# Seven-for-eight up product from the third chunk on, with the cell's steps placed anew beside it

## The chip, the cores and the metric

The kernel runs on one core of a Trainium2 chip. The core has a matrix engine (TensorE, PE in the profile; its weight loads are listed as PEld), three engines for element-wise work (VectorE or DVE, ScalarE or ACT, GpSimd or POOL), and a queue engine (SyncE or SP) that starts most of the DMA transfers. The engines run at the same time, each takes its instructions in order, and they wait for each other by semaphores. The metric is the device time of one execution in microseconds (us); all times here are in us unless marked ns.

## The reference

An mLSTM cell over 4 batches, 8 heads, 768 steps and head dimension 40, and then a feed-forward layer with the activation h·cos(h) over the 3072 rows of 320 that come out of it.

```python
def _attn_ref(q, k, v, i_gate, f_gate, o_gate):
    for t in range(S):
        m_new = np.maximum(f_gate[:, :, t] + m, i_gate[:, :, t])
        f_stab = np.exp(f_gate[:, :, t] + m - m_new)
        i_stab = np.exp(i_gate[:, :, t] - m_new)
        C = f_stab * C + i_stab * (v_t outer k_t)
        n = f_stab * n + i_stab * k_t
        h_tilde = C @ q_t
        denom = np.maximum(np.abs(n . q_t), 1.0)
        y[:, :, t] = sigmoid(o_gate[:, :, t]) * h_tilde / denom

def _moe_ref(x, w_in, w_out):       # x (3072, 320), w_in (320, 2048), w_out (2048, 320)
    h = x @ w_in
    g = h * np.cos(h)
    return (g @ w_out).astype(np.float32)
```

The loop body is shortened here: indices that only spread a value over dimensions are left out.

## The kernel before

**Tiling.** The 768 steps are cut into NC = 6 chunks of C = 128. A *cell* is one chunk of one batch with all eight heads; cells are numbered n = chunk · 4 + batch, 24 in all. Within a cell the recurrence is written as a masked product: scores (keys times queries), weighed with exponentials of the gates, values, and a state that goes on to the next chunk. The feed-forward layer works on the finished chunk: 512 rows (4 batches of 128) by 2048 columns of w_in, in NF / 2 = 8 *up slots* of two blocks of 128 columns. Everything is float32. A float32 matmul shows as two records in the profile.

**The order.** It is written out by hand. `both_parts(c, b)` (line 1265) lays chunk c's up slots 2b and 2b + 1 beside cell n = (c + 1) · 4 + b, which belongs to the next chunk. Two slots with what lies beside them are a *period* here: its first part (i = 0) is the even half, its second (i = 1) the odd half. A chunk has four periods, b = 0 to 3. For c = 5 there is no cell left, and the cells beside c = 4 (n = 20 to 23) no longer add to the state: no `seam`, `fade` and `state` there.

**A slot** (class `Up`, line 697): two banks of 128 by 512 in PSUM get two products each over 128 rows of x (line 715) and one over the 64 remaining rows, the *low rows* (line 709); the two low products use the two halves of the array side by side. Odd slots do the low rows first. Then cos is taken as a sine: ScalarE rounds (`near`, line 723), VectorE takes the rest (`rest`, 726), ScalarE the sine (`sin`, 731), VectorE multiplies by h and 2π (`gate`, 735). e = 0 and 1 are the two banks.

**Seven for eight.** The last chunk (`fast = NC - 1`, line 742) uses `UpFast` (line 769): the product of two blocks of columns with two halves of the rows over two blocks of x, eight products of 256 columns, is done in seven from sums of weights (`up_weight_sums`) and of x (`x_sums`, GpSimd, before the chunk). Four products fill the banks; ScalarE copies both banks out (lines 788, 789); two *filling* products of the down layer (`fill_in`, from f2 = 2 on) lie between; three more products and the low rows go on top. Three adds of the copies (797 and 799 on GpSimd, 798 on VectorE), then two *bank adds* on VectorE (800, 802) give h.

**The down layer.** From chunk 1 on it is a product of the same kind, from sums of the gated values (`sums`, lines 868 to 871, VectorE) and sums of w_out. `down_slot` (line 1031) runs a quota of its products behind each slot: 12 of the chunk before at f2 = 0, 16 *late* ones at f2 = 1, 14 at f2 = 2 to 7 (less two filling ones). `combine_first`, `combine` and `combine_late` add the parts up into output tiles.

**The cell's steps in a period before.** Even half: `scores` right behind the low rows; `weigh` (536) on VectorE; `decay` (448), the eight exponentials of the next cell on ScalarE; behind the slot's down products `values` (556 to 565) and `seam` (the state's increments, 667); then `normalize_turned`, the division on VectorE, which starts with line 583 and ends with 604 and writes the next chunk's x; `fade` (650, GpSimd). Odd half: `state` (692) ahead of the gates, `weigh_k`, and at its end `turn_blocks` (508), two transposes on VectorE that make the next cell's keys and queries for its `scores`, and `scale_q` (512, GpSimd). The exponentials, the sigmoid and the sine are in different tables of ScalarE, so a switch shows as a table load; `sin_next` loads the sine's early.

The end of the even half and of the odd one before, cut:

```python
            down_slot(c, f2)
            if cell and i == 0:
                values(n)
                seam(n)
                normalize_turned(n)
                fade(n)
                sin_next()
            if f2 == 0 and c > 1:
                for p in range(2):
                    combine(c - 1, p)
            if i == 1:
                turn_blocks(n + 1)
                scale_q(n + 1)
```

Of the kernel before, what the change touches and what calls it, by code (L numbers as in the profile page):

```python
# [29 lines left out]
def kernel(  # L30
# [410 lines left out]
    def decay(n):  # L441
        c, b = divmod(n, B)
        if n < B:
            nc.scalar.activation(out=Es[n], in_=Es[n], func=AF.Exp, scale=-1.0)
            return
        for h in range(H):
            g = b * H + h
            nc.scalar.activation(out=Es[n][:, h], in_=Es[n][:, h], func=AF.Exp, scale=-1.0, bias=tab[:, c, 0, g:g + 1])  # L448
# [248 lines left out]
    class Up:  # L697
# [35 lines left out]
        def gate(self, e):  # L733
            g = gp.tile([128, B * C], FP, name="g", tag="g")
            nc.vector.scalar_tensor_tensor(out=g, in0=self.pu[e], scalar=TWO_PI, in1=self.n[e].bitcast(FP),  # L735
                                           op0=OP.mult, op1=OP.mult)
            gs[self.c, 2 * self.f2 + e] = g
# [4 lines left out]
    fast = NC - 1  # L742
    Sw, Tx = {}, {}

    def up_weight_sums(part):

        tt = nc.gpsimd.tensor_tensor
        if part == 0:
            S1, S2, S4, S3 = Sw.setdefault(0, [*(room[:, i] for i in range(3)), blocks[:, FREE_AT:FREE_AT + NF // 2]])
            tt(out=S1, in0=A21, in1=A22, op=OP.add)  # L750
            tt(out=S2, in0=S1, in1=A11, op=OP.subtract)
        else:
            S1, S2, S4, S3 = Sw[0]
            tt(out=S3, in0=A11, in1=A21, op=OP.subtract)
            tt(out=S4, in0=A12, in1=S2, op=OP.subtract)

# [4 lines left out]
    def x_sums(c):  # L761
        T1, T2, T4 = Tx[c] = pe.tile([128, H, C], FP, name="Tx", tag="E")[:, 0:3 * B // 2].rearrange("p (k b) t -> k p b t", k=3)
# [6 lines left out]
    class UpFast(Up):  # L769


        def __init__(self, c, f2, fill):
# [14 lines left out]
            s = pe.tile([128, H, C], FP, name="Sx", tag="E").rearrange("p (k b) t -> p k (b t)", k=4)  # L787
# [10 lines left out]
            nc.vector.tensor_tensor(out=s[:, 0], in0=s[:, 0], in1=s[:, 3], op=OP.add)  # L798
            nc.gpsimd.tensor_tensor(out=s[:, 3], in0=s[:, 1], in1=s[:, 2], op=OP.add)
            nc.vector.tensor_tensor(out=b0[:, second], in0=b0[:, second], in1=s[:, 0], op=OP.add)  # L800
            h = s[:, 0:4:3]
            nc.vector.tensor_tensor(out=h, in0=b1.rearrange("p (k n) -> p k n", k=2), in1=h, op=OP.add)
            self.n = [p3.tile([128, B * C], I32, name="n", tag="n") for _ in range(2)]
            self.h = h

        def near(self, e):
            if e == 0:
                return super().near(e)
            nc.scalar.activation(out=self.n[e].rearrange("p (k n) -> p k n", k=2), in_=self.h, func=AF.Copy, bias=0.25)

        def rest(self, e):
            if e == 0:
                return super().rest(e)
            n = self.n[e].rearrange("p (k n) -> p k n", k=2)
            nc.vector.scalar_tensor_tensor(out=n.bitcast(FP), in0=self.h, scalar=0.25, in1=n, op0=OP.add, op1=OP.subtract)

        def gate(self, e):
            if e == 0:
                return super().gate(e)
            g = gp.tile([128, B * C], FP, name="g", tag="g")  # L820
            nc.vector.scalar_tensor_tensor(out=g.rearrange("p (k n) -> p k n", k=2), in0=self.h, scalar=TWO_PI,
                                           in1=self.n[e].rearrange("p (k n) -> p k n", k=2).bitcast(FP), op0=OP.mult, op1=OP.mult)
            gs[self.c, 2 * self.f2 + e] = g

    def down(c, f2):
# [6 lines left out]
        for f, b in order:  # L832
            nc.tensor.matmul(po[c][b], gs[c, f][:, ts(b, C)], w_out_sb[:, f], start=(f == 0), stop=(f == NF - 1))  # L833
            if f == NF - 1:
                o = out_tile()
                nc.scalar.copy(out=o, in_=po[c][b])
# [4 lines left out]
    T, acc, late, outs_of = [None] * 3, {}, {}, {}  # L841

# [19 lines left out]
    def sums(c, k):  # L862
# [4 lines left out]
        tt = nc.vector.tensor_tensor  # L867
        tt(out=S2_D1, in0=G0[:, :, 1], in1=G1[:, :, 1], op=OP.add)
        tt(out=S0_S1, in0=S2_D1, in1=G0[:, :, 0], op=OP.subtract)
        tt(out=S3_D4, in0=G1[:, :, 0], in1=S0_S1, op=OP.subtract)  # L870
        tt(out=G0[:, :, 1], in0=G0[:, :, 0], in1=G0[:, :, 1], op=OP.subtract)
# [9 lines left out]
    def products(c, k):  # L881
# [6 lines left out]
        made = [(X0, 0, G0[:, 0, 0], B11), (X0, 1, G1[:, 0, 0], B21), (X0, 2, S[:, 0], T2),  # L888
                (Y0, 0, G0[:, 0, 1], T3), (Y0, 1, G1[:, 0, 1], T4), (Y0, 2, S[:, 2], T1),
                (Y1, 2, S[:, 3], B22),  # L890
                (X1, 0, G0[:, 1, 0], B11), (X1, 1, G1[:, 1, 0], B21), (X1, 2, S[:, 1], T2),
                (Y1, 0, G0[:, 1, 1], T3), (Y1, 1, G1[:, 1, 1], T4)]
# [56 lines left out]
    def combine_last():  # L949
        c = NC - 1  # L950
        X0, X1, Y0, Y1 = acc[c]
        tt = nc.vector.tensor_tensor
        lo, hi = slice(0, HALF), slice(HALF, DM)

        def spread_first(X):
            o = [out_tile() for _ in range(2)]
            nc.scalar.copy(out=o[1][:, lo], in_=X[:, 0])
            tt(out=o[0].rearrange("q (h n) -> q h n", h=2), in0=X[:, 1:3], in1=o[1][:, lo].unsqueeze(1).to_broadcast([128, 2, HALF]), op=OP.add)
# [3 lines left out]
        tt(out=o[1][:, hi], in0=Y0[:, 0], in1=o[0][:, hi], op=OP.add)  # L962
        tt(out=o[1].rearrange("q (h n) -> q h n", h=2), in0=Y0[:, 1:3], in1=o[1][:, hi].unsqueeze(1).to_broadcast([128, 2, HALF]), op=OP.add)
        out_to(c, 1, o[1])
        tt(out=o[0][:, hi], in0=Y0[:, 2], in1=o[0][:, hi], op=OP.add)
        p = spread_first(X1)
        tt(out=o[0][:, hi], in0=Y1[:, 1], in1=o[0][:, hi], op=OP.add)
        out_to(c, 0, o[0])
        o, L = p, late[c]
        tt(out=o[1][:, lo], in0=Y1[:, 0], in1=o[0][:, hi], op=OP.add)  # L970
        tt(out=o[1][:, hi], in0=L[:, 0], in1=o[1][:, lo], op=OP.add)
        tt(out=o[0][:, hi], in0=L[:, 0], in1=o[0][:, hi], op=OP.add)
        tt(out=o[0][:, hi], in0=L[:, 1], in1=o[0][:, hi], op=OP.add)
        out_to(c, 2, o[0])
        tt(out=o[1][:, lo], in0=own[c], in1=o[1][:, lo], op=OP.add)
# [12 lines left out]
    def combine_first(c, p):  # L988

        o = outs_of[c, p] = [out_tile() for _ in range(2)]  # L990
        nc.scalar.copy(out=o[1][:, 0:HALF], in_=acc[c][p][:, 0])

    def combine(c, p):

        X0, X1, Y0, Y1 = acc[c]
        X, Y = (X0, Y0) if p == 0 else (X1, Y1)
        tt = nc.vector.tensor_tensor
        o = outs_of[c, p]
        tt(out=o[0].rearrange("q (h n) -> q h n", h=2), in0=X[:, 1:3], in1=o[1][:, 0:HALF].unsqueeze(1).to_broadcast([128, 2, HALF]), op=OP.add)
        if p == 0:  # L1000
            tt(out=o[1][:, HALF:DM], in0=Y[:, 0], in1=o[0][:, HALF:DM], op=OP.add)
            tt(out=o[1].rearrange("q (h n) -> q h n", h=2), in0=Y[:, 1:3], in1=o[1][:, HALF:DM].unsqueeze(1).to_broadcast([128, 2, HALF]), op=OP.add)
            tt(out=o[0][:, HALF:DM], in0=Y[:, 2], in1=o[0][:, HALF:DM], op=OP.add)
            tt(out=o[0][:, HALF:DM], in0=Y1[:, 2], in1=o[0][:, HALF:DM], op=OP.add)
            for e in range(2):
                out_to(c, e, o[e])
        else:
            tt(out=o[1][:, HALF:DM], in0=Y[:, 0], in1=o[0][:, HALF:DM], op=OP.add)
            tt(out=o[1][:, 0:HALF], in0=Y[:, 1], in1=o[1][:, HALF:DM], op=OP.add)

    def combine_late(c):
        tt = nc.vector.tensor_tensor
        o, L = outs_of[c, 1], late[c]
        tt(out=o[0][:, HALF:DM], in0=L[:, 0], in1=o[0][:, HALF:DM], op=OP.add)
        tt(out=o[1][:, HALF:DM], in0=L[:, 0], in1=o[1][:, HALF:DM], op=OP.add)
        tt(out=o[0][:, HALF:DM], in0=L[:, 1], in1=o[0][:, HALF:DM], op=OP.add)
# [6 lines left out]

    def fill_in(c, f2):

# [388 lines left out]
```

## Time and profile before

| | us |
|---|---|
| median of 3 runs | 523.0 (521.36 to 523.67) |
| the profiled execution | 521.93 |
| its span, first to last instruction | 520.2 |
| TensorE clock granted | 1.00 of full speed |

The span is cut into stretches by the start of a chunk's first up product. Columns: length, busy time of TensorE, VectorE, ScalarE, GpSimd.

| stretch | us | PE | DVE | ACT | POOL |
|---|---|---|---|---|---|
| chunk 2 (204.58 to 284.79) | 80.21 | 80.21 | 65.03 | 44.72 | 18.45 |
| chunk 5 and the last products (443.01 to 508.69) | 65.68 | 65.35 | 48.17 | 28.83 | 11.80 |

A busy time is the sum of an engine's instructions in the stretch, with overlaps counted once. TensorE's ends are modelled, and a matmul's record overlaps the next one's; what a product costs is read from the distance between starts. Chunks 3 and 4 are shown in the prediction.

### The profile page before, as it was taken

To read this page: it belongs to the slowest core of one execution; us is meant where nothing else is said; L and a number is where in the kernel's file an instruction comes from. 1 tells how busy PE (TensorE), PEld (TensorE's weight loads), DVE (VectorE), ACT (ScalarE), POOL (GpSimd) and SP (SyncE) were. 2 spreads that over 40 slices of the span, in tenths; PEclk is the share of its full clock that TensorE was granted. 3 is DMA by queue.
4 is the path that set the end of the run, shared out by engine and by line. 5 is a ranking of instruction groups with operands and counts; after the bars stand their busy time and mean duration, and the time that the engine had idled before them with its cause. 6 is when DMAs were issued, how large, how long until landed. Compare 5 with 4: busy or idle time off the path is not lost.

```text
span 520.2 us, 10481 instructions
## 1 busy us (share of the span) xinstructions
PE 504.5 (97%) x3894; PEld 353.1 (68%) x3894; DVE 411.8 (79%) x854; ACT 296.9 (57%) x570; POOL 167.8 (32%) x231
## 2 busy tenths in 40 slices
PE   6999898989999999999999999999999999999997
PEld 4874564545676676776677677667667667787876
DVE  5799998787778788897777897867888767786765
ACT  2889896765854647644546735526836522343531
POOL 7534655442934522311311311311114124112120
PEclk9999999999999999999999999999999999999999
DMA  9989969793666527337337337236331000010001
GB/s 137 205 223 239 266 137 247 190 247 96 126 186 136 127 73 137 93 107 137 112 88 137 93 94 150 80 104 134 86 99 39 1 6 7 2 50 1 1 1 52
DMA packets 101284, 57.84 MB, mean 111 GB/s; under 512 B 63520, under 2 KB 93824, under 8 KB 101232
## 3 DMA queue, kind: packets, MB, share of 16 engines
q1 hardware_dynamic: 97696, 55.48, 45.6%
q10 hardware_dynamic: 3392, 1.49, 1.2%
q8 instruction: 31, 0.51, 0.4%
q0 software_dynamic: 144, 0.18, 0.1%
q14 instruction: 21, 0.17, 0.1%
HBM read 51.71 MB, written 4.11 MB: 107 GB/s over the span
## 4 chain that ended last, share of the span: by engine, by line
PE 84%; DMA 6%; DVE 3%; SPq 3%; ACT 2%; POOL 1%; issue 1%; DVEq 0%; POOLq 0%; ACTq 0%
PE acc L981 25%; PE pup L715 23%; PE pup L709 7%; PE pup L780 5%; PE late L981 4%; DMA bits<-in_moe_w_out_dram 4%; PE po L833 3%; PE ps L530 3%; PE vt L565 2%; PE vt L556 2%; PE pup L796 2%; PE pu L667 1%; PE ph L546 1%; PE pw L1064 1%; SPq L381 1%
## 5 line engine op out<-in xcount | busy, mean ns | idle before, releaser
L715 PE MATMUL pup<-xT,w_in_sb 128*128 128x512 f32 x320 | 146.4, 600 | 2.7 <-DVE g L735 2.4
L723 ACT ACTIVATE n<-pup 128x512 int32<-128x512 f32 x88 | 49.8, 593 | 158.0 <-PE pup L709 86.8
L715 PEld LDWEIGHTS pup<-xT,w_in_sb 128*128 128x128 f32 x320 | 57.8, 189 | 77.3 <-issue 75.5
L726 DVE SCALAR_TENSOR_TENSOR n<-pup,n 128x512 f32<-128x512 f32 x88 | 58.2, 687 | 56.3 <-ACT n L723 54.9
L512 POOL TENSOR_TENSOR qG<-t,G 128x512 f32<-128x512 f32 x20 | 25.5, 1276 | 151.8 <-DVE t L508 140.7
L731 ACT ACTIVATE n<-n 128x512 f32<-128x512 f32 x96 | 58.0, 628 | 21.3 <-DVE n L726 11.2
L735 DVE SCALAR_TENSOR_TENSOR g<-pup,n 128x512 f32<-128x512 f32 x88 | 56.8, 684 | 2.4 <-ACT n L731 1.7
L981 PE MATMUL acc<-w_out_sb,g 128*128 128x160 f32 x320 | 58.4, 303 | 0.0
L981 PE MATMUL acc<-T,g 128*128 128x160 f32 x304 | 55.0, 300 | 0.0
L981 PEld LDWEIGHTS acc<-w_out_sb,g 128*128 128x128 f32 x320 | 48.1, 190 | 4.4 <-issue 2.7
L448 ACT ACTIVATE E<-E,tab 128x128 f32<-128x128 f32 x160 | 49.0, 388 | 3.1 <-POOL E L434 2.9
L709 PE MATMUL pup<-xL,w_in_l 64*128 64x512 f32 x160 | 45.2, 641 | 2.9 <-POOL w_in_l L187 2.9
L981 PEld LDWEIGHTS acc<-T,g 128*128 128x128 f32 x304 | 45.8, 190 | 1.8 <-issue 1.4
L650 POOL TENSOR_TENSOR st<-st,tab 40x128 f32<-40x128 f32 x64 | 24.3, 391 | 59.6 <-PE vt L565 58.4
L833 PE MATMUL po<-w_out_sb,g 128*128 128x320 f32 x128 | 36.2, 436 | 1.7 <-POOL w_out_sb L187 1.7
L981 PE MATMUL acc<-T,blocks 128*128 128x160 f32 x160 | 35.4, 303 | 0.0
L833 PEld LDWEIGHTS po<-w_out_sb,g 128*128 128x128 f32 x128 | 24.0, 190 | 13.0 <-POOL w_out_sb L187 2.1
L530 PEld LDWEIGHTS ps<-t,t 40*128 40x128 f32 (+1 forms) x384 | 24.8, 187 | 10.5 <-issue 6.3
L981 PEld LDWEIGHTS acc<-T,blocks 128*128 128x128 f32 x160 | 26.1, 190 | 6.0 <-issue 6.0
L536 DVE TENSOR_TENSOR E<-ps,E 128x512 f32<-128x512 f32 x46 | 29.4, 680 | 0.0
L981 PE MATMUL acc<-w_out_sb,blocks 128*128 128x160 f32 x160 | 28.7, 299 | 0.0
L1196 ACT ACT_TABLE_LOAD x21 | 26.9, 1283 | 0.4
(227 smaller groups left out, 873.0 us busy)
## 6 DMA issues: line engine op xcount, KB each, us to landing
E<-M_d SPq DMA_DIRECT2D x21, 512.0 KB
qr<-in_q_dram SPq DMA_DIRECT2D x72, 80.0 KB
kr<-in_k_dram SPq DMA_DIRECT2D x72, 80.0 KB
bits<-in_moe_w_out_dram SPq DMA_DIRECT2D x8, 640.0 KB
G<-G_d SPq DMA_DIRECT2D x18, 256.0 KB
blocks<-in_moe_w_in_dram SPq DMA_DIRECT2D x32, 128.0 KB
out_dram<-o_sb SPq DMA_DIRECT2D x23, 160.0 KB
o<-in_o_gate_dram SPq DMA_DIRECT2D x40, 80.0 KB
```

The lines of the kernel that those rows point to most:

```text
L448: nc.scalar.activation(out=Es[n][:, h], in_=Es[n][:, h], func=AF.Exp, scale=-1.0, bias=tab[:, c, 0, g:g + 1])
L530: nc.tensor.matmul(ps[j][:, p], kT[r, p], qT[r, p], start=True, stop=True)
L536: nc.vector.tensor_tensor(out=w, in0=pss[n][j], in1=w, op=OP.mult)
L709: nc.tensor.matmul(pu, w_in_l[r, f2], xL[c][r].rearrange("p b t -> p (b t)"), start=ahead, stop=not ahead)
L715: nc.tensor.matmul(pu.rearrange("p (b t) -> p b t", b=B), w_in_sb[:, i, ts(2 * f2 + e, 128)], xT[c][:, i:NK * B:NK], start=(i == 0 and not ...
L723: nc.scalar.activation(out=self.n[e], in_=self.pu[e], func=AF.Copy, bias=0.25)
L726: nc.vector.scalar_tensor_tensor(out=self.n[e].bitcast(FP), in0=self.pu[e], scalar=0.25, in1=self.n[e], op0=OP.add, op1=OP.subtract)
L731: nc.scalar.activation(out=r, in_=r, func=AF.Sin, scale=TWO_PI_DOWN)
L735: nc.vector.scalar_tensor_tensor(out=g, in0=self.pu[e], scalar=TWO_PI, in1=self.n[e].bitcast(FP), op0=OP.mult, op1=OP.mult)
L833: nc.tensor.matmul(po[c][b], gs[c, f][:, ts(b, C)], w_out_sb[:, f], start=(f == 0), stop=(f == NF - 1))
L981: nc.tensor.matmul(a, lhs, rhs, start=start, stop=stop)
L1196: nc.scalar.activation(out=spot, in_=spot, func=AF.Sin)
```

## The change

It has these parts; the diff below is cut to them.

1. `fast` becomes 2: chunks 2 to 5 use `UpFast`, in a new function `both_parts_fast`. The weight sums are made in chunk 1 (three parts), one of them in place of its own summand; the sums of x get a tile of their own (`x_room`) and are made in the last odd half of each chunk. Filling products are run at f2 = 0 and from 2 on.
2. In the new function the next cell's scores stand in the odd half, right behind the low rows, and are weighed there; values and increments stand in the even half right behind the low rows. The division, the state, the sums and `turn_blocks` follow the even half's gates in this order. The first period (c = 2, b = 0) has its own scores in the even half as well.
3. `decay` is split: six exponentials (three for b = 0) in the even half, the others in the odd half behind the slot's copies. The sigmoid for the next chunk is taken at b = 0 behind the slot's copies.
4. In `UpFast` all three adds of the copies are on GpSimd, h of the second bank is written to the tile of the gated value, and the second gate is on GpSimd (except the very last).
5. `sums` of f2 = 0 and 1 are on GpSimd in chunks 2 to 4. The order of its four operations changes.
6. 2π is left out of the gates and multiplied in when the output is put together. `combine` is split in `combine_x` (even half, behind the division) and `combine_y` (end of the odd half); `combine_late` moves into the next even half, ahead of the gates. Products of the down layer are taken in another order.

```diff
+    def decay(n, heads=range(H)):
@@ class Up
-            nc.vector.scalar_tensor_tensor(out=g, in0=self.pu[e], scalar=TWO_PI, in1=self.n[e].bitcast(FP),
-                                           op0=OP.mult, op1=OP.mult)
+            nc.vector.tensor_tensor(out=g, in0=self.pu[e], in1=self.n[e].bitcast(FP), op=OP.mult)
@@
-    fast = NC - 1
+    fast = 2
+    x_room = const.tile([128, 3 * B // 2, C], FP, name="x_room")
@@ up_weight_sums
+        S1, S2, S4 = (room[:, i] for i in range(3))
+        Sw[0] = S1, S2, S4, A21
         if part == 0:
             tt(out=S1, in0=A21, in1=A22, op=OP.add)
             tt(out=S2, in0=S1, in1=A11, op=OP.subtract)
+        elif part == 1:
             tt(out=S4, in0=A12, in1=S2, op=OP.subtract)
+        r = ((), range(0, 4), range(4, NF // 2))[part]
+        if r:
+            r = slice(r[0], r[-1] + 1)
+            tt(out=A21[:, r], in0=A11[:, r], in1=A21[:, r], op=OP.subtract)
@@ UpFast
-            nc.vector.tensor_tensor(out=s[:, 0], in0=s[:, 0], in1=s[:, 3], op=OP.add)
+            nc.gpsimd.tensor_tensor(out=s[:, 0], in0=s[:, 0], in1=s[:, 3], op=OP.add)
...
+            self.g = gp.tile([128, B * C], FP, name="g", tag="g")
+            nc.vector.tensor_tensor(out=self.g.rearrange("p (k n) -> p k n", k=2), in0=b1.rearrange("p (k n) -> p k n", k=2), in1=s[:, 0:4:3], op=OP.add)
+            self.pu[1] = self.g
...
+            tt = nc.vector.tensor_tensor if (self.c, self.f2) == (NC - 1, NF // 2 - 1) else nc.gpsimd.tensor_tensor
+            tt(out=self.g, in0=self.g, in1=self.n[e].bitcast(FP), op=OP.mult)
@@ sums
-    def sums(c, k):
+    def sums(c, k, engine=nc.vector):
         tt(out=S2_D1, in0=G0[:, :, 1], in1=G1[:, :, 1], op=OP.add)
+        tt(out=G0[:, :, 1], in0=G0[:, :, 0], in1=G0[:, :, 1], op=OP.subtract)
         tt(out=S0_S1, in0=S2_D1, in1=G0[:, :, 0], op=OP.subtract)
         tt(out=S3_D4, in0=G1[:, :, 0], in1=S0_S1, op=OP.subtract)
-        tt(out=G0[:, :, 1], in0=G0[:, :, 0], in1=G0[:, :, 1], op=OP.subtract)
@@ combining
+    def add_turns(out, in0, in1):
+        nc.vector.scalar_tensor_tensor(out=out, in0=in0, scalar=TWO_PI, in1=in1, op0=OP.mult, op1=OP.add)
...
+    def filled(c, f2):
+        return c >= fast and f2 != 1
@@ both_parts, c = 1
-                if c == fast - 1 and b in (0, 2):
-                    up_weight_sums(b // 2)
+                if c == fast - 1 and b > 0:
+                    up_weight_sums(b - 1)
+                if c == fast - 1 and b == B - 1:
+                    x_sums(c + 1)
+    def both_parts_fast(c, b):
+        n = (c + 1) * B + b
+        cell, follows = n < N, n + 1 < N
+        first = (c, b) == (fast, 0)
+        ahead = 3 if b == 0 else H - 2
+        pool = nc.gpsimd if cell else nc.vector
+        for i in range(2):
+            f2 = 2 * b + i
+            up = UpFast(c, f2, lambda: fill_in(c, f2))
+            if cell and i == 0:
+                if first:
+                    scores(n)
+                    scale_q(n)
+                else:
+                    values(n)
+                    seam(n)
+                if b == 0:
+                    sigmoid(c + 1)
+                if follows:
+                    decay_exponents(n + 1)
+            if cell and i == 1:
+                if follows:
+                    decay(n + 1, range(ahead, H))
+                    sin_next()
+                    scores(n + 1)
...
+                if b == B - 1:
+                    x_sums(c + 1)
+                elif follows:
+                    weigh_k(n + 1)
+                    odd_values(n + 1)
+                    scale_q(n + 1)
+            for e in range(2):
+                up.near(e)
+            for e in range(2):
+                up.rest(e)
+            if first and i == 0:
+                weigh(n)
+            if f2 == 2:
+                combine_late(c - 1)
+            if cell and i == 0 and not first:
+                fade(n)
+            if cell and i == 1:
+                seam_out(n)
+            for e in range(2):
+                up.sin(e)
+                up.gate(e)
+            if f2 == 0:
+                sums(c, 0, pool)
+            if f2 == 2:
+                sums(c, 1, pool)
+            down_slot(c, f2)
+            if f2 == 0:
+                for p in range(2):
+                    combine_first(c - 1, p)
+            if cell and i == 0:
+                if follows:
+                    decay(n + 1, range(ahead))
+                if first:
+                    values(n)
+                    seam(n)
+                    fade(n)
+                normalize_turned(n)
...
+            if f2 == 0:
+                for p in range(2):
+                    combine_x(c - 1, p)
+            if i == 0:
+                if cell:
+                    state(n)
+                if f2 > 0:
+                    sums(c, f2)
+                if follows:
+                    turn_blocks(n + 1)
+            if i == 1:
+                if follows:
...
+                    weigh(n + 1)
+                if b == 0:
+                    combine_y(c - 1)
+                else:
+                    sums(c, f2)
```

## The prediction

> **What bounds the kernel now.** First the busy times and the chain of waits of the page.
>
> ```profile
> PE 504.5 (97%) x3894; PEld 353.1 (68%) x3894; DVE 411.8 (79%) x854; ACT 296.9 (57%) x570; POOL 167.8 (32%) x231
> PE 84%; DMA 6%; DVE 3%; SPq 3%; ACT 2%; POOL 1%; issue 1%; DVEq 0%; POOLq 0%; ACTq 0%
> ```
>
> TensorE sets the end. Next the busy times by chunk, cut where a chunk's first up product starts (columns: stretch, length, busy time of PE, PEld, DVE, ACT, POOL with counts, clock, DMA share, GB/s).
>
> ```profile
> 284.79:365.00 80.21, 80.21 (x673) 56.44 (x673) 64.53 (x140) 44.19 (x85) 17.79 (x29) 1.00 0.47 111
> 365.00:443.01 78.01, 78.01 (x608) 54.70 (x608) 62.13 (x124) 37.70 (x73) 21.05 (x16) 1.00 0.13 37
> ```
>
> In chunks 3 and 4 (chunk 2 reads like 3: 80.21) TensorE has no gap, so work taken from it is time, if nothing else makes it wait. VectorE is at 80%: its order decides that. So I read both in order of time, first in chunk 3 (start, length, engine, line, operation).
>
> ```profile
> 314.26 0.43 PE L556 MATMUL vt<-E,vs 128*32 128x128 f32 x8
> 316.40 1.13 PE L709 MATMUL pup<-xL,w_in_l 64*128 64x512 f32 x4
> ...
> 329.29 1.06 PE L530 MATMUL ps<-t,t 40*128 40x128 f32 x16
> 330.28 0.54 PE L981 MATMUL acc<-T,g 128*128 128x160 f32 x2
> ```
>
> ```profile
> 322.44 0.86 DVE L692 TENSOR_TENSOR st<-st,pu 40x128 f32<-40x128 f32 x4
> 323.33 1.29 DVE L735 SCALAR_TENSOR_TENSOR g<-pup,n 128x512 f32<-128x512 f32 x2
> 324.65 0.42 DVE L868 TENSOR_TENSOR blocks<-g 128x256 f32<-128x256 f32 x1
> ...
> 326.25 1.10 DVE L508 STREAM_TRANSPOSE t<-qr 128x512 f32<-128x512 f32 x1
> 327.18 1.10 DVE L508 STREAM_TRANSPOSE t<-kr 128x512 f32<-128x512 f32 x1
> ...
> 336.08 0.33 DVE L583 STREAM_TRANSPOSE vt<-vt 128x128 f32<-128x128 f32 x1 [0.31 <-PE vt L565]
> ...
> 338.65 0.56 DVE L604 TENSOR_TENSOR xT<-vt,oT 128x384 f32<-128x384 f32 x1
> ```
>
> The blocks turned by line 508 are ready at 328.28, the scores that read them start at 329.29: one microsecond to spare. Then chunk 5, which has the seven products already but no cell beside them.
>
> ```profile
> 460.20 0.59 PE L780 MATMUL pup<-Tx,room 128*128 128x256 f32 x2
> 461.92 0.71 PE L981 MATMUL acc<-w_out_sb,g 128*128 128x160 f32 x4
> 462.47 0.59 PE L780 MATMUL pup<-Tx,w_in_sb 128*128 128x256 f32 x2
> 463.86 1.13 PE L796 MATMUL pup<-xL,w_in_l 64*128 64x512 f32 x4
> 464.92 0.54 PE L981 MATMUL acc<-T,blocks 128*128 128x160 f32 x2
> 465.02 0.43 DVE L800 TENSOR_TENSOR pup<-pup,Sx 128x256 f32<-128x256 f32 x1 [0.82 <-PE pup L796]
> 467.64 0.68 DVE L735 SCALAR_TENSOR_TENSOR g<-pup,n 128x512 f32<-128x512 f32 x1
> ```
>
> One up slot takes 460.20 to 464.92. VectorE can start on it 0.10 after its low rows, and starts the first gate 2.72 after them, because ScalarE's rounding and sine lie between.
>
> **What TensorE saves.** A 512-column product takes 0.857 (eight records in 3.43), a 256-column one 0.43 (460.20 to 461.92 is four). Seven for eight halves saves 0.43 a slot, 24 slots in chunks 2 to 4: 10.3. New pieces of TensorE, from the rows: up slot with two filling products U = 4.72 (4.17 without); 12 down products C = 3.36 (24 records take 3.26, plus 0.10 for the first pair behind low rows), ten 2.82, the 16 late ones 4.45; values and increments V = 2.14 (314.26 to 316.40); scores S = 1.05 (0.99 and 1.09 in two periods). A period is two slots: V + C + U = 10.22 to the end of the odd slot's low rows, then S + C + U = 9.13, together 19.35 against 80.21 / 4 = 20.05. Chunk 2 pays S twice at its start (78.4), chunk 3 takes 77.4, chunk 4, without increments (0.47) and with no next cell at its end, 74.5: 230.3 against 238.4. Chunk 5's first slot now is filled (7.54 against 8.05, 443.01 to 451.06): −0.5. With no new wait the gain is 8.6.
>
> **What VectorE must do before the scores.** TensorE takes instructions in order. Behind the odd slot's low rows now stand the next cell's scores, which read what turn_blocks makes, and behind them the down products. turn_blocks is the last VectorE step of the even half. Counted from the end of the even slot's low rows: bank adds, two rests and the first gate, ready for the next step at 2.72 + 0.62 = 3.34; division, 336.08 to 338.65 and 0.48 to the next, 3.05; state 0.89 (322.44 to 323.33); the sums 1.60 (324.65 to 326.25; the new order of the four has the same two dependent pairs); the two transposes 0.93 + 1.10 = 2.03. Sum 10.91, and 0.06 for the signal: 10.97. Before, the division ran ahead of the rests, while the product was still under way; that cover is gone. TensorE is there at 10.22, so it waits 0.75, and the period is 10.97 + 9.13 = 20.10: the saving is eaten. This holds for b = 2 and 3. For b = 1 combine_late stands ahead of the first gate (three adds of 0.32 which took 0.8 from first start to end): 11.77 and 20.90.
>
> **b = 0.** Here ScalarE is late too. It does the sigmoid after the slot's copies (load 1.28, 1.49 of work, 283.42 to 286.20) and loads the sine's table (1.28) after the second rounding, which ends 2.08 after the low rows: sines from 3.38, first gate at 4.05 instead of 2.72, second sine out at 4.56. The two copies of combine_first wait for the ten products (4.96) and end at 5.55; exponential's table 6.83; three exponentials, 0.31 apart, to 7.75; then the odd slot's copies, which its fifth and sixth product need: 8.35 and 8.87. TensorE, without filling there, is at 6.77. The odd low rows end at 8.93 + 0.96 + 1.06 = 10.95 instead of 9.22. VectorE: 4.05 + 0.62 + 3.05, two combine_x adds 0.90, state 0.89, transposes 2.03 = 11.54. With S + 4.45 + U = 10.22 behind it, 21.8. The first such period (chunk 2) has its scores and two weighings in front, so the values end at 5.6 and the transposes at 12.5: 22.8. In chunk 4, without state: 20.9.
>
> **Sum.** Chunk 2: 22.8 + 20.9 + 2 × 20.1 = 83.9 (+3.7). Chunk 3: 82.9 (+2.7). Chunk 4: 20.9 + 20.0 + 19.2 + 17.8 = 77.9 (−0.1). Chunk 5 −0.5. Together +5.8: span 520.2 to 526.0, the profiled execution's 521.93 to 527.7. It lies 1.1 under the median of 523.0, so I write 528.
>
> **Edits at nothing.** GpSimd gets per slot three adds of 0.72 (line 797) and a gate at line 512's 1.27, twice a chunk four sums (3.1), and x_sums (four, 0.77 apart, 3.1): some 36 on top of 18 of 80. The adds start 2.6 into a slot, behind the copies, and end at 4.85, just as the bank adds may start: hidden by the slot itself, 0.2 late if each takes 0.94 (line 797's longest). The gate ends about 4.8, sums need it at 7.3. Weight sums of 2.37 each fall in chunk 1, where GpSimd is idle 60%; the last half-sum and x_sums end 7.1 into the last slot, where the second product comes at 7.2. Without that cover they'd cost 1 once. Copies for b > 0: six exponentials end at 6.6, the first copy is possible at 6.6. Scaling by 2π at the output: same shapes, same rows (0.68, 0.32). Moved DMAs: two output stores a chunk go half a period later on SP, with loads behind them that are read a period later. The low rows' input is issued after the odd slot's rounding, as before.
>
> **Unknown sizes.** The wait at the scores is 0.75 by the rows; at best 0 (the block 0.75 shorter), at worst with GpSimd's traffic: line 871, a sum, took 0.62 instead of 0.42 beside line 650 on GpSimd. The four sums now run beside the three adds: 0 to 0.8 a period. I take 0, since line 871's median over 40 is 0.418. [...]
>
> **Rivals.** A, the other side: VectorE's block ends in time, because TensorE's part is longer or a step is shorter by 0.8 to 1.5; only b = 0's late copies cost (0.3, 1.7, 1.6), so −8.6 + 3.6 = −5.0: 517 (513 without them). For it: VectorE has 15% idle over a chunk. Against: that idle time lies in the odd half. It decides from a block under 10.2. B, contention: eight periods with sums ahead of the transposes, 0.8 each, 6.4 more: 534. C, half the waits: 0.4 less in each of 11 periods, 4.4 less: 523.3, no difference. That the seven products save nothing is excluded by chunk 5's 0.43 pitch.
>
> **How the numbers follow.** Forecast 0.55 (own range 525 to 531), A 0.20, B 0.12, C 0.13. No change is what lies within 0.5%, 520.4 to 525.6. Faster: A and the edge of C, 0.22; same: most of C and the forecast's low edge, 0.15; slower 0.63. Range 515.5 to 534: A's and B's own times in it.
>
> **What would show it.** Up slots of 4.7 in chunks 2 to 4. Right: score matmuls or their weight loads that wait for the transposes, 0.7 to 1.6 each, longest for b = 0 and 1; bank products that wait for the copies at b = 0; periods near 20.1. Wrong: scores right behind the low rows, periods near 19.4, and a chunk under 79.

## The result and the profile after

The changed kernel takes 547.4 us (median of four, 545.8 to 549.8), the kernel before beside it 523.3 (521.4 to 524.7): ratio 1.047, 95% interval 1.041 to 1.052. The forecast was 528.0 with a range up to 534: the direction is right, the size is not. First the page after: busy times, the row of TensorE's granted clock (40 slices, in tenths), the chain of waits.

```profile
PE 508.8 (94%) x4038; PEld 385.3 (71%) x4038; DVE 417.1 (77%) x839; ACT 326.4 (60%) x614; POOL 296.9 (55%) x379
...
PEclk9889999999999999898999999989999899999999
...
PE 60%; DVE 13%; DMA 10%; POOL 6%; ACT 5%; issue 4%; SPq 2%; DVEq 0%; ACTq 0%; POOLq 0%
```

TensorE's share of the chain fell from 84% to 60%, VectorE's rose from 3% to 13%: the end is now set by VectorE in places. The clock row has 8s, where a slice ran partly at half clock. Then the busy times from chunk 2 on, cut at each chunk's first up product, the last line ending with the last slot of chunk 5 (columns as in the prediction: stretch, length, PE, PEld, DVE, ACT, POOL, clock, DMA share, GB/s).

```profile
206.01:295.59 89.58, 82.83 (x739) 68.49 (x738) 70.33 (x143) 54.08 (x99) 53.79 (x72) 0.96 0.44 107
295.59:383.96 88.37, 79.99 (x723) 65.90 (x721) 70.45 (x141) 53.75 (x99) 57.12 (x75) 0.98 0.41 100
383.96:464.62 80.66, 77.19 (x642) 63.16 (x641) 60.61 (x120) 47.98 (x88) 44.87 (x53) 0.98 0.09 27
464.62:532.38 67.76, 65.78 (x371) 52.66 (x370) 42.56 (x84) 29.93 (x51) 29.17 (x33) 1.00 0.03 11
```

| stretch | before | forecast | after |
|---|---|---|---|
| start of chunk 2 | 204.6 | 204.6 | 206.0 |
| chunk 2 | 80.2 | 83.9 | 89.6 |
| chunk 3 | 80.2 | 82.9 | 88.4 |
| chunk 4 | 78.0 | 77.9 | 80.7 |
| chunk 5 to the end of its last slot | 65.7 | 65.2 | 67.8 |
| from there to the end | 11.5 | 11.5 | 11.7 |
| span | 520.2 | 526.0 | 544.0 |

TensorE had no gap in chunk 3 before; now it is busy for 80.0 of 88.4, and part of that time is spent at a lower clock (0.98 over the chunk). One odd half, period b = 1 of chunk 2, in order of time on TensorE:

```profile
240.85 0.59 PE L783 MATMUL pup<-x_room,room 128*128 128x256 f32 x2
...
244.53 1.13 PE L799 MATMUL pup<-xL,w_in_l 64*128 64x512 f32 x4
248.30 1.38 PE L530 MATMUL ps<-t,t 40*128 40x128 f32 x16 [2.64 <-DVE t L508]
249.61 0.90 PE L974 MATMUL acc<-w_out_sb,g 128*128 128x160 f32 x2
...
250.83 1.27 PE L974 MATMUL acc<-T,g 128*128 128x160 f32 x4
...
253.30 0.71 PE L974 MATMUL acc<-w_out_sb,g 128*128 128x160 f32 x4
```

The up slot takes 240.85 to 245.6, 4.7 as forecast. Then the scores (line 530) wait 2.64 for the transposes (line 508). Behind them four records of down products (two products of one shape) take 1.27 at 250.83, and four such records take 0.71 at 253.30. VectorE and GpSimd in the same stretch, the second fence GpSimd's:

```profile
238.66 0.68 DVE L735 TENSOR_TENSOR g<-pup,n 128x512 f32<-128x512 f32 x1
...
242.32 0.86 DVE L692 TENSOR_TENSOR st<-st,pu 40x128 f32<-40x128 f32 x4
243.22 0.43 DVE L863 TENSOR_TENSOR blocks<-g 128x256 f32<-128x256 f32 x1
243.68 0.83 DVE L864 TENSOR_TENSOR g<-g 128x256 f32<-128x256 f32 x1
244.44 0.94 DVE L865 TENSOR_TENSOR blocks<-blocks,g 128x256 f32<-128x256 f32 x1
245.41 0.83 DVE L866 TENSOR_TENSOR blocks<-g,blocks 128x256 f32<-128x256 f32 x1
246.16 1.07 DVE L508 STREAM_TRANSPOSE t<-qr 128x512 f32<-128x512 f32 x1
247.09 1.06 DVE L508 STREAM_TRANSPOSE t<-kr 128x512 f32<-128x512 f32 x1
```

```profile
243.50 0.73 POOL L800 TENSOR_TENSOR blocks<-blocks 128x256 f32<-128x256 f32 x1 [0.38 <-ACT blocks L792]
244.31 0.79 POOL L801 TENSOR_TENSOR blocks<-blocks 128x256 f32<-128x256 f32 x1
245.17 0.79 POOL L802 TENSOR_TENSOR blocks<-blocks 128x256 f32<-128x256 f32 x1
```

The four sums take 3.02 from first start to end; ahead of the transposes of chunk 3 in the kernel before, with GpSimd idle, they took 1.68 (324.65 to 326.33). The first, which starts ahead of GpSimd's first add, has its 0.43; the other three end at 244.51, 245.38 and 246.24, each 0.28 after one of GpSimd's adds (244.23, 245.10, 245.96), the one that was under way when the sum began.

The clock is seen by stretches: the products behind two long waits, then those behind a short one (third line).

```profile
224.40:230.60 6.20, 6.20 (x36) 6.11 (x33) 5.16 (x11) 1.78 (x3) 2.16 (x2) 0.72 0.08 24
249.60:254.40 4.80, 4.80 (x27) 4.79 (x26) 4.25 (x9) 1.42 (x3) 1.27 (x1) 0.70 0.99 166
270.53:275.30 4.77, 4.77 (x42) 4.62 (x43) 4.19 (x8) 2.38 (x4) 2.50 (x2) 1.00 0.34 91
```

A granted clock of 0.72 over 6.20 is some 3.4 at half clock. Four such stretches lie in chunks 2 to 4 (from 225.2, 249.1, 358.3 and 423.2), each 3.41 long at a granted clock of 0.50. They begin 0.8 to 1.8 after a wait at the scores has ended, waits that the timeline shows as 1.76, 2.64, 2.00 and 1.84; each costs 1.7, half its length.

Where the 18.0 beyond the forecast span come from: the scores' waits add up to 17.5 (their distance to the low rows, less the usual 0.96) where the forecast had 10.8: +6.7. Half clock: +6.8. Chunk 5: +2.6. The start of chunk 2: +1.4; in this execution the first cells ran at half clock from 23.8 to 30.7. Three of the runs below have the same chunk 1 and no such stretch (transposes first, TensorE kept busy, combine_late moved), and there chunk 2 starts at 202.8 to 203.1; so this term is not a cost of the change. Copies at b = 0: 1.49 and 1.24, together 0.9 less than forecast. What is left, 1.4, is spread.

### The profile page after: what moved, and what is told of

Its sections match the earlier page's. It is cut to its first block, busy times and chain, and to the rows that moved or that the text cites. A ratio compares the mean times of both kernels' runs of the same rounds, so it can differ in the third digit from the quotient of the medians.

```text
span 544.0 us, 11055 instructions
## 1 busy us (share of the span) xinstructions
PE 508.8 (94%) x4038; PEld 385.3 (71%) x4038; DVE 417.1 (77%) x839; ACT 326.4 (60%) x614; POOL 296.9 (55%) x379
## 3 DMA queue, kind: packets, MB, share of 16 engines
q10 hardware_dynamic: 3392, 1.49, 1.1%
## 4 chain that ended last, share of the span: by engine, by line
PE 60%; DVE 13%; DMA 10%; POOL 6%; ACT 5%; issue 4%; SPq 2%; DVEq 0%; ACTq 0%; POOLq 0%
PE acc L974 18%; PE pup L783 12%; PE pup L715 6%; DMA bits<-in_moe_w_out_dram 5%; PE late L974 4%; PE pup L799 4%; PE ps L530 4%; DVE t L508 3%; PE po L824 2%; PE pup L709 2%; ACT n L723 2%; DVE n L726 1%; DMA xL<-xT 1%; DMA E<-M_d 1%; PE vt L565 1%
## 5 line engine op out<-in xcount | busy, mean ns | idle before, releaser
L813 POOL TENSOR_TENSOR g<-g,n 128x512 f32<-128x512 f32 x31 | 39.4, 1272 | 61.2 <-ACT n L731 61.2
L800 POOL TENSOR_TENSOR blocks<-blocks 128x256 f32<-128x256 f32 x32 | 25.6, 799 | 68.9 <-ACT blocks L792 68.8
L715 PE MATMUL pup<-xT,w_in_sb 128*128 128x512 f32 x128 | 58.8, 602 | 1.8 <-DVE g L735 1.6
L726 DVE SCALAR_TENSOR_TENSOR n<-pup,n 128x512 f32<-128x512 f32 x64 | 43.1, 689 | 21.9 <-ACT n L723 19.3
L803 DVE TENSOR_TENSOR pup<-pup,blocks 128x256 f32<-128x256 f32 x32 | 13.9, 434 | 56.4 <-PE pup L799 55.5
L783 PE MATMUL pup<-xT,w_in_sb 128*128 128x256 f32 x192 | 52.9, 384 | 0.4 <-ACT blocks L792 0.2
L735 DVE TENSOR_TENSOR g<-pup,n 128x512 f32<-128x512 f32 x64 | 42.6, 687 | 8.5 <-ACT n L731 7.9
L791 ACT COPY blocks<-pup 128x512 f32<-128x512 f32 x32 | 18.7, 583 | 50.1 <-PE pup L783 49.5
L530 PE MATMUL ps<-t,t 40*128 40x128 f32 (+1 forms) x384 | 28.2, 287 | 15.7 <-DVE t L508 15.7
L783 PE MATMUL pup<-x_room,room 128*128 128x256 f32 x128 | 38.2, 380 | 0.0
```

The costliest lines, as they stand in the source:

```text
L530: nc.tensor.matmul(ps[j][:, p], kT[r, p], qT[r, p], start=True, stop=True)
L715: nc.tensor.matmul(pu.rearrange("p (b t) -> p b t", b=B), w_in_sb[:, i, ts(2 * f2 + e, 128)], xT[c][:, i:NK * B:NK], start=(i == 0 and not ...
L726: nc.vector.scalar_tensor_tensor(out=self.n[e].bitcast(FP), in0=self.pu[e], scalar=0.25, in1=self.n[e], op0=OP.add, op1=OP.subtract)
L735: nc.vector.tensor_tensor(out=g, in0=self.pu[e], in1=self.n[e].bitcast(FP), op=OP.mult)
L783: nc.tensor.matmul(bank[:, part].rearrange("p (b t) -> p b t", b=B // 2), w[:, f2], x, start=start, stop=stop, skip_group_check=True)
L800: nc.gpsimd.tensor_tensor(out=s[:, 1], in0=s[:, 1], in1=s[:, 0], op=OP.add)
```

## The experiments

Theory W: the scores wait because VectorE's block ahead of the transposes is too long, and the half clock follows from TensorE standing still. Theory V: the work on GpSimd slows VectorE wherever it stands, and its order matters little. The first four kernels each change one thing of the changed kernel; the kernel before took 522.4 (520.8 to 522.9) beside them.

**The transposes ahead of the sums.**

```diff
-                if f2 > 0:
-                    sums(c, f2)
                 if follows:
                     turn_blocks(n + 1)
+                if f2 > 0:
+                    sums(c, f2)
```

> The changed kernel with the transposes put ahead of the even half's sums. Theory W (the scores wait for VectorE's serial block, sums included): the transposes are ready 1.6 to 3.0 us earlier in the eight periods with sums ahead of them; their waits (13.5 us in the changed kernel) nearly vanish and with them three of the four stretches at half clock (5 us), so 528 to 534 us. Rival V (VectorE as a whole is the bound once it has GpSimd beside it, order does not matter): 543 to 549 us.

535.2 (two runs, 534.5 and 535.9), ratio 1.025 (1.019 to 1.031): 12 us of 24 come back from the order alone, against V; but 1.2 more than W allowed. The scores' wait is gone except for the first period of chunk 2 (1.74). In its place, in order of time:

```profile
269.11 0.70 PE L783 MATMUL pup<-xT,w_in_sb 128*128 128x256 f32 x2 [1.33 <-DVE g L735]
...
302.73 1.22 PE L783 MATMUL pup<-x_room,w_in_sb 128*128 128x256 f32 x2 [1.82 <-ACT blocks L791]
```

The sums now push the odd slot's bank adds and gate, and the next up slot waits for the bank that this gate reads; at b = 0 the copies are as late as ever. The wait has moved one slot on, at half its size. Half clock still follows in each first period of a chunk (from 220.6, 302.5 and 387.8, 3.41 each).

**GpSimd's three adds left out** (the up product's second halves are then not complete).

```diff
-            nc.gpsimd.tensor_tensor(out=s[:, 1], in0=s[:, 1], in1=s[:, 0], op=OP.add)
-            nc.gpsimd.tensor_tensor(out=s[:, 0], in0=s[:, 0], in1=s[:, 3], op=OP.add)
-            nc.gpsimd.tensor_tensor(out=s[:, 3], in0=s[:, 1], in1=s[:, 2], op=OP.add)
```

> The changed kernel without the three adds of the bank copies on GpSimd; the sums of the copies are left out of h. Theory C (the sums on VectorE take 0.83 instead of 0.42 us because these adds run beside them): all sums ahead of the transposes at 0.42 to 0.46 us, waits at the scores shorter by 0.4 to 1.6 us in eight periods, 533 to 541 us. Rival (the sums are slow by their own operands): sums still at 0.83, 544 to 549 us.

540.0 (two runs, 539.95 and 539.98), ratio 1.034 (1.029 to 1.040): 7.4 less, as contention would have it, though the bank adds also no longer wait for the third add, so the time alone doesn't separate the two. The sums themselves do. In b = 2, with nothing on GpSimd beside them, they take 1.68; in b = 3 of the same chunk the four x_sums stand beside them, and VectorE shows

```profile
283.40 0.43 DVE L860 TENSOR_TENSOR blocks<-g 128x256 f32<-128x256 f32 x1
283.86 0.84 DVE L861 TENSOR_TENSOR g<-g 128x256 f32<-128x256 f32 x1
284.62 0.94 DVE L862 TENSOR_TENSOR blocks<-blocks,g 128x256 f32<-128x256 f32 x1
285.60 0.83 DVE L863 TENSOR_TENSOR blocks<-g,blocks 128x256 f32<-128x256 f32 x1
```

3.03 for the same four instructions, whatever GpSimd adds up beside them. The expected 0.42 to 0.46 for all sums came in three of the eight halves only; in the others (2.10 to 3.03 for the four) other work of GpSimd had come to stand beside them.

**TensorE kept busy at the waits**: two 512-column products into the scores' bank, overwritten by the scores.

```diff
-                    scores(n + 1)
+                    scores(n + 1, 2)
...
+        for _ in range(busy):
+            nc.tensor.matmul(ps[0].rearrange("p h t -> p (h t)"), w_in_sb[:, 0, 0:128], w_in_sb[:, 0, 0:512], start=True, stop=True)
```

> The changed kernel with two products of 512 columns, whose result is overwritten, ahead of each scores that stand in the odd half, so that TensorE computes during the wait. Theory H (the half clock follows TensorE's idle time): no stretch at half clock in chunks 2 to 4, the 12 or 16 products behind the scores at 0.27 us each everywhere; 6.8 us less for that, up to 3 us more where 1.7 us of products exceed the wait: 541 to 545 us. Rival (the products behind the scores are slow for their operands or for the engines beside them): stretches at half clock or slow products stay, 546 to 550 us.

542.8 (541.7 and 544.0), ratio 1.040 (1.032 to 1.047), although 1.7 of needless products stand in each of 11 periods, most of it inside the waits that were there anyway. The slots with the scores of b = 0 and b = 1 in chunk 2, waits included, read

```profile
213.70:226.00 12.30, 12.13 (x73) 8.81 (x72) 11.43 (x25) 7.56 (x17) 9.34 (x14) 1.00 0.16 50
236.20:248.10 11.90, 11.24 (x69) 8.31 (x68) 11.12 (x20) 6.66 (x14) 7.90 (x10) 1.00 0.87 198
```

The clock is 1.00 in these and in all other slots of chunks 2 to 4 (0.999 over the run, against 0.98). So in chunks 2 to 4 the half clock follows from TensorE standing still and not from what the changed kernel computes.

**combine_late at the end of b = 0** instead of behind the rests of b = 1.

```diff
-            if f2 == 2:
-                combine_late(c - 1)
...
                     combine_y(c - 1)
+                    combine_late(c - 1)
```

> The changed kernel with combine_late at the end of b = 0's odd half (behind combine_y) instead of ahead of the gates of b = 1. Theory W: b = 1's waits at the scores 0.8 us shorter (three chunks), the wait of 1.8 us in chunk 5 gone, perhaps one or two stretches at half clock less: 537 to 543 us. Rival (combine_late was hidden there): 544 to 549 us.

537.5 (536.1 and 538.8), ratio 1.030 (1.022 to 1.038), in W's range and below the rival's. The edit takes away the wait that chunk 5 had beyond the forecast. In the changed kernel the timeline of TensorE and VectorE there reads

```profile
487.35 0.71 PE L974 MATMUL acc<-w_out_sb,blocks 128*128 128x160 f32 x4
489.02 0.78 DVE L836 SCALAR_TENSOR_TENSOR o_sb<-late,o_sb 128x160 f32<-128x160 f32 x3
489.85 0.81 PE L974 MATMUL acc<-w_out_sb,g 128*128 128x160 f32 x4 [1.79 <-DVE o_sb L836]
```

Chunk 5 makes its products in another order. Seven of them run without a wait (the last two are the first line); the eighth, by the code's order the first into X1, waits until combine_late, which stands behind the rests, has ended its last add, 1.79 too late. The timeline does not say which bank ties the two together. With the edit this wait is gone; in b = 1 the scores still wait, 1.97, 1.97 and 1.65.

**The first sums of every even half on GpSimd**, on top of the last edit; those of f2 = 1 go to VectorE behind combine_late. The next four kernels build on one another.

```diff
-            if f2 == 0:
-                sums(c, 0, pool)
-            if f2 == 2:
-                sums(c, 1, pool)
+            if f2 == 0 or cell and i == 0:
+                sums(c, f2, pool)
...
-                if f2 > 0:
+                if f2 > 0 and not cell:
                     sums(c, f2)
...
                     combine_late(c - 1)
-                else:
-                    sums(c, f2)
+                sums(c, f2)
```

> Builds on the run with combine_late one half earlier (537.5 us): the first sums of every even half go to GpSimd, right behind its gate, and those of the half-period f2 = 1 go to VectorE's idle time behind combine_late; the transposes then stand directly behind the state update. Theory W (scores wait because VectorE's block ahead of the transposes is too long, and TensorE's half clock follows such waits): the block is shorter by the four sums (1.7 to 2.7 us), the scores' wait stays only in the first period of a chunk, b = 0 keeps its late copies (1.2 to 1.5 us): 523 to 531 us. Theory V (GpSimd and VectorE slow one another down, whichever of them has the sums): the sums' 2.9 us on GpSimd stretch the other block and push the odd half's adds, 533 to 540 us.

523.2 (median of ten, 521.1 to 526.4), ratio 1.003 (1.000 to 1.005): 14 less than the run before, at the bottom of W's range, and V is out. In b = 1 of chunk 2 VectorE now reads

```profile
241.55 0.86 DVE L692 TENSOR_TENSOR st<-st,pu 40x128 f32<-40x128 f32 x4
242.44 1.13 DVE L508 STREAM_TRANSPOSE t<-qr 128x512 f32<-128x512 f32 x1
243.41 1.11 DVE L508 STREAM_TRANSPOSE t<-kr 128x512 f32<-128x512 f32 x1
245.63 0.43 DVE L803 TENSOR_TENSOR pup<-pup,blocks 128x256 f32<-128x256 f32 x1 [1.11 <-PE pup L799]
```

State, transposes, then 1.11 in which VectorE waits for TensorE. The order of who waits has turned. Left are b = 0's waits: 1.77 and 1.14 at the scores, 1.82, 1.24 and, in b = 1 of chunk 4, 1.52 at the copies.

**The sigmoid back in the last odd half of the chunk before**, and b = 0's transposes ahead of combine_x.

```diff
-                if b == 0:
-                    sigmoid(c + 1)
...
+                    if b == B - 1 and c < NC - 2:
+                        sigmoid(c + 2)
                     sin_next()
...
+            if (c, f2) == (1, NF // 2 - 1):
+                sigmoid(c + 2)
+                sin_next()
...
-            if f2 == 0:
-                for p in range(2):
-                    combine_x(c - 1, p)
             if i == 0:
...
                     turn_blocks(n + 1)
+                if b == 0:
+                    for p in range(2):
+                        combine_x(c - 1, p)
```

> As the run with the sums on GpSimd, and the sigmoid goes out of the even half of b = 0 to the last odd half of the chunk before (one table load and three activations, 2.85 us, and the sine's table load 1.28 us leave the path to the first gate), and the transposes go ahead of the two combine_x of b = 0 (0.88 us). Theory W: the late copies (1.2 to 1.5 us) and the scores' wait of b = 0 go, with the half clock behind it: 4 to 9 us less than the run with the sums on GpSimd alone, 514 to 522 us, under the kernel before. Rival: the sigmoid pushes the odd half's sines and the next slot's copies, as it did in the kernel before; then the two runs agree within 2 us.

522.9 (median of ten, 520.2 to 525.3), ratio 1.001 (0.999 to 1.003): the rival. The scores' waits shrink to one of 1.08, but the copies still wait 1.71, 1.46, 1.04 and 1.53. The first of these is new: at the end of chunk 1 the sigmoid, put behind the gates, holds up the copies of chunk 2's first slot. Those of b = 0 remain because three exponentials with their table load (1.28 in the changed kernel) stand ahead of them.

**Three more terms off the path**: the sums of f2 = 1 on GpSimd, combine_first behind the copies of b = 0's odd half, chunk 1's sigmoid ahead of that half's rounding.

```diff
-            if f2 == 0 or cell and i == 0:
+            if f2 == 0 or cell and (i == 0 or f2 == 1):
                 sums(c, f2, pool)
...
+    def between(c, f2, cell):
+        fill_in(c, f2)
+        if f2 == 1 and cell:
+            for p in range(2):
+                combine_first(c - 1, p)
+            for p in range(2):
+                combine_x(c - 1, p)
...
-            up = UpFast(c, f2, lambda: fill_in(c, f2))
+            up = UpFast(c, f2, lambda: between(c, f2, cell))
...
+                if (c, f2) == (1, NF // 2 - 1):
+                    sigmoid(c + 2)
+                    sin_next()
             for e in range(2):
                 up.near(e)
```

> As the run with the sigmoid moved back, with three terms that its trace shows as still on the path taken away: the sums of f2 = 1 go from VectorE (3.86 us behind combine_late, with VectorE busy without a gap up to the next gate) to GpSimd right behind its gate; the two combine_first (0.48 us) go behind the copies of b = 0's odd half on ScalarE; the first of the moved sigmoids goes ahead of the odd half's first halves of the gate. Theory W (what is left over the forecast is these waits for the copies: 1.71, 1.46, 1.04 and 1.53 us in that run): the third product's wait in b = 1 of chunk 4 and at the start of chunk 2 goes and those of b = 0 fall by 0.5 us: 3.5 to 5 us less, 517.5 to 519.5 us against 522 us before. Rival (the work has no room left on any engine, each wait removed comes back elsewhere): 521 to 524 us.

521.7 (median of twelve, 520.8 to 524.0), ratio 1.000 (0.998 to 1.001): a miss, in the rival's range. The waits named did shrink (1.53 to 0.40, 1.46 to 1.07, 1.04 to 0.65), but the 1.71 came back elsewhere at the same size: the sigmoid now delays chunk 1's last gate, and chunk 2's first product waits 1.71 for the bank that this gate reads.

**Filling everywhere and a shorter way to that gate**: two of the twelve products left over from the chunk before fill the pause at f2 = 1; one exponential instead of three ahead of its copies; in chunk 1's last period no sine table load before the sigmoid, and the state behind the gates.

```diff
-        return c >= fast and f2 != 1
+        return c >= fast
...
-            run(products_of(c if f2 > 0 else c - 1), FILL)
+            run(products_of(c if f2 > 1 else c - 1), FILL)
...
-                run(made_of[c - 1], 12 - FILL * filled(c, f2))
+                run(made_of[c - 1], 12 - 2 * FILL * filled(c, f2))
...
-        ahead = 3 if b == 0 else H - 2
+        ahead = 1 if b == 0 else H - 2
...
-                sin_next()
+                if (c, b) != (1, B - 1):
+                    sin_next()
...
-                if cell:
+                if cell and (c, b) != (1, B - 1):
                     state(n)
...
                     up.gate(e)
+                if (c, b) == (1, B - 1):
+                    state(n)
```

> As the run before it, and three edits for the waits that are left there (1.71 at the start of chunk 2; 1.07, 0.65 for the copies and 1.08, 0.50 for the transposes in b = 0; 4.6 us more with 0.54 a chunk of products that do not fill): two of the twelve products left over from the chunk before fill the pause for the copies of f2 = 1 too (0.54 a chunk), only one exponential instead of three stands ahead of those copies (0.6), and in the last period of chunk 1 the sigmoid goes without a sine table load before it (1.28) and the state update stands behind the gates (0.86). Theory W (what keeps the kernel from the forecast of 514 to 517 are single waits in b = 0): 3 to 4.5 us less, 517 to 519 us against 522, ratio 0.990 to 0.995. Rival (no room left): within 1 us of the run before, 521 to 523 us.

519.2 (median of six, 518.5 to 520.2) against 522.4 (median of ten), ratio 0.9946 (0.9929 to 0.9964): half a per cent faster than the kernel before, 0.2 above W's range. The edits came together, so what each is worth is not shown. Its chunks 2 to 4:

```profile
202.70:282.90 80.20, 78.89 (x737) 65.56 (x738) 63.26 (x133) 51.83 (x97) 61.23 (x83) 1.00 0.50 115
282.90:362.30 79.40, 77.81 (x721) 64.48 (x721) 62.56 (x128) 52.29 (x99) 64.16 (x86) 1.00 0.48 114
362.30:438.90 76.60, 75.63 (x643) 61.88 (x642) 57.48 (x111) 44.56 (x85) 53.67 (x65) 1.00 0.09 29
```

and a period of it, by the first products of three slots:

```profile
254.62 0.59 PE L783 MATMUL pup<-x_room,room 128*128 128x256 f32 x2
263.62 0.59 PE L783 MATMUL pup<-x_room,room 128*128 128x256 f32 x2
273.86 0.59 PE L783 MATMUL pup<-x_room,room 128*128 128x256 f32 x2
```

19.24 for two slots, with no wait in them over 0.3: the period that the forecast would have had without waits was 19.35, before it was 20.05. Chunks 2 to 4 take 236.2, against 238.4 before and 230.3 by the forecast without waits. Of these 5.9, 3.3 are waits, nearly all in b = 0 (1.08 and 1.05 at the scores, 0.47 and, in b = 1 of chunk 4, 0.73 at the copies); the rest was not followed. 1.9 more come ahead of chunk 2, whose start before was 204.6; the changed kernel has 1.5 to 1.8 of that already where its first cells keep the full clock.

## Why the prediction was wrong in size

*What TensorE saves*: right. The up slot took 4.74 for U = 4.72; from the even slot's low rows to the odd slot's end 10.2 for V + C + U = 10.22; a period without waits 19.24 for 19.35. The saving is there, and shows in the last kernel.

*What VectorE must do before the scores*: right as a mechanism. In b = 1 of chunk 2 its block ran from 235.35 to 248.15, 12.8 for 11.77. Up to the end of the state it measured 7.87 for 8.08, the transposes 2.0 for 2.03. The sums' term is the one that failed: 2.94 to the first transpose, for 1.60.

*Unknown sizes*: here is the first step that failed. The sums beside GpSimd's adds were bounded at 0 to 0.8 a period, and 0 was taken "since line 871's median over 40 is 0.418". 27 of these 40 records ran with GpSimd idle, so the median said little of the case asked about. Of the 13 that overlapped with GpSimd four took 0.62 or 0.63, all beside line 650, where the prediction names one; two of another sum, line 869, took 1.19 and 1.20 beside line 434. Over the eight even halves with sums on VectorE, in chunks 2 to 4, they took 3.02, 2.09, 2.09, 3.03, 2.62, 2.09, 3.01 and 1.67, together 6.2 more than 1.68 each. Rival B said 6.4 and 534. It had chance 0.12; its size was right, and it accounts for most of the 6.7 at the scores; its time fell short, since it had no term for the clock either. The bank adds of line 803, with one input in PSUM, kept their 0.43 beside GpSimd in 31 of 32 records and took 0.47 in one.

*The clock*: no step of the prediction spoke of it. Every wait was priced as its own length. Four waits carried 1.7 more, 6.8 in all, of which the run with TensorE kept busy shows that they go with the idle time. With B and the clock the sum would have been 541.

*Chunk 5*, forecast −0.5, measured +2.1. The prediction has no term for a product there that waits for combine_late. 1.79 of it is that wait, shown by the run that moved combine_late.

*b = 0*: right. The copies were late at b = 0 by 1.49 and 1.24, forecast 1.7 and 1.6; at chunk 2's start they were in time, forecast 0.3.

*Edits at nothing*: GpSimd's adds were hidden where the prediction looked, on GpSimd and at the bank adds. What they cost they cost on VectorE. That rival A's condition can be met was borne out: with a block under 10.2 the scores don't wait. Its 517 was not reached, but 519.2 was, by other edits.

*The last step of the sum*: 527.7 with the 1.1 that the prediction names is 528.8, not 528. Nothing hangs on it.

## What to carry to other kernels

When work moves to a second engine, price the neighbours too: look up what their instructions took in just those records that ran beside such work, the longest among them, and not the median over all. Where a matrix engine with a serial block ahead of it gains a little, ask what it does while it waits: a wait can cost its own length and a stretch of half clock behind it (here 1.7 more, behind four of the waits). And a change that saves on the bounding engine is worth only what the next longest chain leaves; here the saving of 0.8 a period showed only when the sums had left VectorE's block, and most of it was still eaten by single waits at the chunks' seams until each of these was taken away.

## What the hardware showed that was not expected

VectorE's sums took 0.42 alone and 0.83 to 0.94 beside GpSimd in the rows above, those of the changed kernel and those of the run without the three adds, where x_sums stand beside them. What a sum loses there is the rest of GpSimd's instruction and not a fixed factor: in the changed kernel's chunk 3 one took 1.49 (from 297.79) beside line 512's 1.47 (from 297.53), and it too ended 0.28 after it. In the profiles of the kernel before and the changed kernel 44 sums began while an instruction of GpSimd had 0.2 or more to go, and each of them ended 0.26 to 0.29 after that instruction. In turn GpSimd's add of line 801 took 0.78 to 0.80 beside a sum (11 records) and 0.72 to 0.73 alone (21).

TensorE's half clock came in steps of time. In the changed kernel's chunks 2 to 4 each stretch lasts 3.41 (in the run with combine_late moved, twice two steps, 6.83), and the second, third and fourth start 23.9, 133.1 and 198.0 after the first, which is 7, 39 and 58 times 3.413, the length that the trace's clock records give for each of the four. In the step just ahead of the four, TensorE was idle for 1.60, 2.61, 2.00 and 1.61. On the same grid the wait of 2.63 in chunk 3, behind which the clock stayed full, falls on two steps with 1.37 and 1.26; one of 2.03 in the run without the adds falls on two with 1.00 and 1.03. So in these runs a wait counted by what one step got of it: 2.63 split in two left the clock full, 1.60 in one step did not. From chunk 2 to the last slot of chunk 5, over all runs, no stretch began behind a step with less than 1.51 idle, one always began from 1.82 up, and in between it went both ways: 1.79 ahead of 491.45 in the changed kernel passed. Idle time is not the whole condition, then. The half clock of the first cells, from 23.8, began behind a step with only 0.26 idle, filled with their small products. What the exact condition is, these runs don't settle.
